# A hand-laid order of some 300 steps laid anew in a fused attention and feed-forward kernel: loads, copies and one PSUM bank with it

## The chip, the core and the metric

The kernel runs on one core of a Trainium2 chip. Its five engines run side by side, each in the order of its own instructions: TensorE (PE) multiplies matrices, VectorE (DVE) and ScalarE (ACT) work element by element, GpSimd (POOL) here issues the loads, and SyncE (SP) issues the stores and the transposes done by DMA. Semaphores order the work between them. The metric is the time of one execution on the device in microseconds; less is better.

## The reference

```
q, k, v: (4, 8, 768, 64)   n_global = 8, n_local = 96
scores = q k^T / 8 - slope[head] * dist,  kept where key < 8 or 0 <= query - key < 96
attn   = softmax(scores) v
x      = attn as (3072, 512)
h      = x @ w_in                     (512 x 2048)
out    = softplus(h) @ w_out          (2048 x 512), float32
```

Each query thus sees the eight global keys of its sequence and a band of 96 keys up to itself. `dist` is the distance, or 96 for a global key outside the band.

## The kernel before

A sequence is cut into six blocks of 128 queries; four sequences make 24 blocks. Block `n` needs the keys of its own block and of the block before. The rows of that earlier block which the band cannot reach are overwritten with the eight global keys and values (`gk`, `gv`), so that two key blocks are enough. The feed-forward part takes tiles of 256 tokens (two blocks), twelve in all, each with eight units of 256 columns of `w_in` (`f`) and eight units of the second product (`o`).

Everything is written as named steps. A step issues instructions on several engines at once, and each engine keeps the order in which the steps issue to it. The names:

- `lq`, `lk`, `lv` load a block (cast to bf16 on the way) from POOL's queue; `wi` and `wo` load weights on the same queue. `w_in` lies in five pieces (`W_IN`): units 0 and 1 alone, then 2-3, 4-5 and 6-7 together.
- `w` multiplies zeros on PE, into a bank that nobody reads. `cq`, `ck` cast the first blocks of q and k, loaded unconverted by SP's and ACT's queues.
- `t` transposes q and k of a block on PE into the bank `tr`, and DVE (or ACT, by a second number) copies them out; `tq`, `tk` do this for block 0, one tensor at a time, through the same bank. From block 8 on `d` lets the DMA transpose (SP).
- `z` writes the bias of a block (blocks 0 to 3) into the score bank by a matmul with the identity; `s` adds the scores; for later blocks `s` is followed by an addition on DVE. `e` is the exp on ACT, `p` the product with v and the division on DVE. The second number is the half of the heads.
- `x` transposes the result on PE into `XT`; `y` lets the DMA do it, on SP's queue.
- `f`: eight matmuls into one of two `hT` banks, then exp and log on ACT. `o`: four matmuls of 512 columns; every fourth is followed by DVE's copy and a store on SP.
- `g` makes POOL wait for a given unit of `f`, so that later loads are not issued too early.

The bias tables `biasA` are made by eight ACT instructions at the start (L177), ahead of every step. The first 304 steps stand in the string `ORDER`; what is left comes after it in the order of computed due times, the same in both kernels. `hT` banks come from the pool `ps2` with two buffers, which some early transposes and products share; `tr` has one.

```
nc.vector.tensor_copy(KT[n - 1][:, :, 0:NG], KT[first_of(n)][:, :, 0:NG])          # gk, L247
nc.vector.tensor_copy(v_t[n - 1][0:NG, :, 0:D], v_t[first_of(n)][0:NG, :, 0:D])    # gv, L251
```

Of the kernel before, what the change touches and what calls it, by code (L numbers as in the profile page):

```python
# [19 lines left out]
def kernel(  # L20
# [82 lines left out]
    def load_w_in(u):  # L103
        f0, f1 = u * CT, (u + W_IN[u]) * CT
        nc.gpsimd.dma_start(  # L105
            w_in_c[u][:], moe_w_in[:, f0:f1].rearrange("(m p) f -> p m f", p=P)
        )
# [64 lines left out]
    ones(2, RV)  # L172


    for half in range(2):
        for j in range(4):
            nc.scalar.mul(  # L177
                biasA[:, half, 2 * j : 2 * j + 2, :], dist_dp[:], -slopes[head_of(half, 2 * j)]
            )
# [27 lines left out]
    def tr_in(tr, j, src):
        for m in range(NPAIR):
            nc.tensor.transpose(  # L209
                tr[:, j, m, :], src[:, 2 * m : 2 * m + 2, :].rearrange("p a b -> p (a b)"), ident[:]  # L210
            )
# [8 lines left out]
    def to_KT(n, tr, copy):  # L220
        KT[n] = work4.tile(
            [P, NPAIR, P], BF16, tag="KT0" if n == first_of(n) else "KT", name="KT"
        )
        copy(KT[n][:], tr[:, 1, :, :])
# [19 lines left out]
    def gk(n):  # L244

        if n % BPB >= 2:
            nc.vector.tensor_copy(KT[n - 1][:, :, 0:NG], KT[first_of(n)][:, :, 0:NG])  # L247

    def gv(n):
        if n % BPB >= 2:  # L250
            nc.vector.tensor_copy(v_t[n - 1][0:NG, :, 0:D], v_t[first_of(n)][0:NG, :, 0:D])  # L251
# [203 lines left out]
    ORDER = """
        w16 cq0 lk1 ck0 lq1 lv0 w2 tq0 lv1 z0.1 w1 lq2 tk0 lk2 z0.0 w1 s0.0 e0.0 lk3 s0.1 t1 lv2 z1.0 lq3 p0.0
        s1.0 e0.1 lv3 z1.1 s1.1 gk2 e1.0 e1.1 t2 gk12 p0.1 p1.0 z2.0 z2.1 s2.0 p1.1 s2.1 gv2 t3 gk3 x0 wi0
        e2.0 wi1 z3.0 wi2 e2.1 x1.1 lq4 p2.0 lk4 lv4 s3.0 p2.1 z3.1 s3.1 e3.0 gv3 e3.1 wi4 x2.1 p3.0 gk4 f0
        p3.1 f1 x3 f8 f9 f2 t4 lk5 gv4 f10 s4.0 f3 lq5 f11 s4.1 wo0 f12 wi6 wo1 t5 f4 e4.0 lv5 wo2 gk5 f5
        wo3 o0 f13 o4 p4.0 e4.1 lq6 s5.0 e5.0 f6 f7 s5.1 e5.1 o1 p4.1 lk6 gv5 o5 g11 y4 g13 f14 p5.0 f15 lv6  # L460
        g7 o2 p5.1 y5 o6 o3 lk7 gk13 o7 lq7 t6 lq8 lq9 o8 lk8 s6.0 g15 e6.0 o9 o10 e6.1 lq10 t7 lv7 d8
        o11 s7.0 lk9 f16 o12 e7.0 lk10 p6.0 e7.1 d9 o13 o14 p6.1 f17 f18 y6 p7.0 o15 f19 gk8 p7.1 f20 s8.0
        lv8 f21 y7 e8.0 gk9 d10 o16 e8.1 o17 gv8 f22 p8.0 g17 s9.0 f23 o18 p8.1 gv9 gk10 e9.0 g19 lv9 f24
        f25 lq11 o19 g21 lv10 e9.1 lk11 d11 g25 f26 lv11 p9.0 s10.0 f27 p9.1 y8 g27 gk11 e10.0 e10.1 g23 o20
        o21 f28 y9 lq12 o22 gv10 f29 lq13 o23 p10.0 f30 lk12 f31 lk13 p10.1 y10 g31 s11.0 g29 gv11 e11.0 d12
        lv12 lk14 o24 e11.1 d13 o25 lq14 f32 o26 p11.0 o27 f33 p11.1 f34 o28 f35 g35 o29 y11 f36 o30 f37
        gv13 s12.0 d14 g33 o31 e12.0 e12.1 f38 p12.0 f39 lv13 s13.0 p12.1 e13.0 o32 lq15 f40 o33 e13.1 f41
        g37 gk14 y12 p13.0 lk15 g39 lk16 f42 d15 lv14 s14.0 e14.0 p13.1 gv12 f43 o34 gv14 f44 y13 lq16 e14.1
        o35 g41 g43 f45 lv15 lk17
    """  # L470
# [98 lines left out]
```

## Time and profile before

| | |
|---|---|
| median of three runs | 215.35 us (214.91 to 216.95) |
| the profiled execution | 215.15 us, of which the profile's span is 213.4 |
| PE busy | 205.5 us (96%) |
| ACT busy | 161.0 us (75%) |
| DVE busy | 109.0 us (51%) |
| POOL busy | 74.2 us (35%) |

The span runs from the first to the last instruction of the program. Of every row of a timeline the first number is the start and the second the duration, both in us; in brackets stands how long the engine was idle before it and what ended the wait. A row of the chain has start and duration, too; a row of groups has the count, the busy time, the mean in ns of one and the idle time before. A row of windows has the stretch, its length, then for each engine (PE, weight loads, DVE, ACT, POOL) its busy time and its instructions, the granted clock, the share of the DMA engines and their GB/s. L12 is line 12 of the kernel. Matmuls are pipelined, so PE starts one before the last one's duration is over.

### The profile page before, as it was taken

The numbers are of one execution on the slowest core, as the hardware profiler recorded it, in microseconds if no ns is written. First come the engines' busy times: TensorE is split into PE (matmuls) and PEld (weight loads), VectorE is DVE, ScalarE is ACT, GpSimd is POOL, SyncE is SP. The second block draws the span as 40 slices with busy tenths as digits, with TensorE's granted clock in tenths as the row PEclk, the third lists the DMA queues.
The fourth block names the chain that finished last, engine by engine and source line by source line (L and its number), as shares of the span: only waits on it lengthen the run. The fifth ranks groups of instructions, "written<-read, shape, count | busy, mean of one in ns | idle before, by whom it ended". The sixth has DMA issues, their size and how long they took to land.

```text
span 213.4 us, 4944 instructions
## 1 busy us (share of the span) xinstructions
PE 205.5 (96%) x1948; PEld 141.3 (66%) x1979; DVE 109.0 (51%) x258; ACT 161.0 (75%) x251; POOL 74.2 (35%) x116
## 2 busy tenths in 40 slices
PE   7999999999998999999999999999999999999994
PEld 2677876646766677677767766666767767666653
DVE  7595436367575656077575663465674663110121
ACT  3778999625898977799978878778878978777700
POOL 8996521880160535325552342352311000000000
PEclk9999999999999999999999999999999999999999
DMA  9999999999999999999999999999992612101112
GB/s 131 153 160 176 189 207 199 173 173 191 181 112 112 126 187 121 162 166 68 136 150 127 187 162 128 140 134 126 136 155 62 93 25 66 60 3 49 49 49 98
DMA packets 111543, 27.33 MB, mean 128 GB/s; under 512 B 103712, under 2 KB 108576, under 8 KB 111520
## 3 DMA queue, kind: packets, MB, share of 16 engines
q0 software_dynamic: 77552, 13.37, 88.2%
q1 hardware_dynamic: 32928, 13.38, 35.9%
q10 hardware_dynamic: 1040, 0.26, 0.5%
q8 instruction: 15, 0.25, 0.5%
q14 instruction: 8, 0.07, 0.1%
HBM read 27.26 MB, written 6.29 MB: 157 GB/s over the span
## 4 chain that ended last, share of the span: by engine, by line
PE 74%; DMA 15%; POOL 7%; issue 2%; DVE 0%; POOLq 0%; DVEq 0%
PE o L414 32%; PE hT L394 32%; DMA k_t<-in_k_dram 8%; DMA w_in<-in_moe_w_in_dram 5%; PE x_ps L343 4%; DMA XT<-xsf 3%; PE s_ps L260 3%; POOL q_t L99 2%; POOL k_t L99 2%; POOL v_t L99 2%; PE o L436 2%; PE s_lo L260 1%; POOL w_in L105 1%; PE tr L209 0%; POOL w_out L110 0%
## 5 line engine op out<-in xcount | busy, mean ns | idle before, releaser
L394 PE MATMUL hT<-XT,w_in 128*128 128x256 bf16 x768 | 98.3, 273 | 1.3 <-DMA XT<-xsf 0.6
L394 PEld LDWEIGHTS <-w_in 128*128 128x128 bf16 x768 | 73.6, 98 | 24.6 <-DVE XT L378 0.7
L414 PE MATMUL o<-w_out,G 128*128 128x512 bf16 x339 | 88.4, 379 | 1.5 <-issue 0.3
L399 ACT ACTIVATE e_sb<-hT 128x512 f32<-128x512 f32 x96 | 56.4, 587 | 23.2 <-PE hT L394 22.5
L400 ACT ACTIVATE G<-e_sb 128x512 bf16<-128x512 f32 x96 | 60.5, 630 | 3.6
L414 PEld LDWEIGHTS <-G 128*128 128x128 bf16 x368 | 33.0, 98 | 26.8
L327 ACT ACTIVATE Pb<-Z 128x1024 bf16<-128x1024 f32 (+1 forms) x40 | 38.9, 983 | 8.9 <-DVE Z L295 4.8
L420 DVE COPY osb<-o 128x512 f32<-128x512 f32 x23 | 15.9, 691 | 37.8 <-PE o L414 37.1
L451 POOL COPY gate_t<-G 1x1 bf16<-1x1 bf16 x32 | 5.7, 178 | 76.1 <-ACT G L400 75.7
L297 DVE TENSOR_TENSOR Z<-s_ps,biasA 128x1024 f32<-128x1024 f32 x19 | 23.2, 1221 | 11.8 <-PE s_ps L260 11.8
L354 DVE RECIPROCAL rcp<-x_ps 128x4 f32<-128x4 f32 x44 | 7.9, 180 | 30.6 <-PE x_ps L343 30.5
L99 POOL DMA_DIRECT2D v_t<-in_v_dram x24 | 21.3, 890 | 5.2 <-PE x_ps L343 2.3
L99 POOL DMA_DIRECT2D q_t<-in_q_dram x23 | 20.6, 898 | 3.5 <-issue 2.4
L99 POOL DMA_DIRECT2D k_t<-in_k_dram x23 | 20.8, 908 | 1.3 <-issue 0.9
L357 DVE TENSOR_TENSOR xsf<-x_ps,rcp 128x256 bf16<-128x256 f32 x44 | 18.7, 424 | 2.4 <-DMA XT<-xsf 0.6
L343 PEld LDWEIGHTS <-Pb 128*128 128x128 bf16 x352 | 16.7, 97 | 3.4 <-issue 0.2
L343 PE MATMUL x_ps<-v_t,Pb 128*128 128x65 bf16 x324 | 17.1, 193 | 0.0
L260 PEld LDWEIGHTS <-KT 64*128 64x128 bf16 x352 | 9.9, 94 | 6.5 <-issue 4.0
L318 DVE TENSOR_TENSOR Z<-s_lo,biasA 128x512 f32<-128x512 f32 x15 | 10.2, 679 | 0.0
L318 DVE TENSOR_TENSOR Z<-o,biasA 128x512 f32<-128x512 f32 x15 | 10.2, 679 | 0.0
L260 PE MATMUL s_ps<-QT,KT 64*128 64x128 bf16 x192 | 9.9, 219 | 0.2
L251 DVE COPY v_t<-v_t 8x512 bf16<-8x512 bf16 x16 | 7.0, 435 | 0.0
(63 smaller groups left out, 93.1 us busy)
## 6 DMA issues: line engine op xcount, KB each, us to landing
out_dram<-osb SPq DMA_DIRECT2D x23, 256.0 KB, 3.7
v_t<-in_v_dram POOLq DMA_DIRECT2D x24, 128.0 KB, 5.2
k_t<-in_k_dram POOLq DMA_DIRECT2D x23, 128.0 KB, 6.1
q_t<-in_q_dram POOLq DMA_DIRECT2D x23, 128.0 KB, 6.1
w_out<-in_moe_w_out_dram POOLq DMA_DIRECT2D x4, 512.0 KB, 14.5
w_in<-in_moe_w_in_dram POOLq DMA_DIRECT2D x3, 512.0 KB, 9.9
w_in<-in_moe_w_in_dram POOLq DMA_DIRECT2D x2, 256.0 KB, 6.0
XT<-xsf SPq DMA_TRANSPOSE x20, 4.7
```

Of the source, the lines that this page charges most:

```text
L99: nc.gpsimd.dma_start(dst[n][:, :, 0:D], src[b, :, i * P : (i + 1) * P, :].rearrange("h s d -> s h d"))
L260: nc.tensor.matmul(dst(4 * sub + 2 * mm + t), KT[n - t][rows, m, :], QT[n][rows, m, :], start=not pre, stop=not pre or (mm == 1 and (t == ...
L297: nc.vector.tensor_tensor(Z[:], s_ps[:], biasA[:, half, :, :], ALU.add)
L318: nc.vector.tensor_tensor(Z[:, regs, :], s_i[:, 0:4:step, :], bias[:, 1, regs, :], ALU.add)
L327: nc.scalar.activation(Pb[:, 0:nreg, :], src, AF.Exp, scale=inv_sqrt)
L343: nc.tensor.matmul(x_b[:, lh, :], Pb[:, r, :], v_t[n - t][:, h, :], start=(t == 0), stop=(t == 1 or first),)
L357: nc.vector.tensor_tensor(xsf[:, h0 : h0 + 4, :], x_b[:, :, 0:D], rcp[:, h0 : h0 + 4][:, :, None].to_broadcast([P, 4, D]), ALU.mult,)
L394: nc.tensor.matmul(hT[:, j, :], w[:, m, fo : fo + P], XT[c][:, m, :], start=(m == 0), stop=(m == KM - 1),)
L399: nc.scalar.activation(e_sb[:], hT[:], AF.Exp)
L400: nc.scalar.activation(G[c][:, 2 * u : 2 * u + 2, :], e_sb[:], AF.Ln, bias=1.0)
L414: nc.tensor.matmul(o[:], G[c][:, 4 * kq + a, ns * P : ns * P + P], w_out_c[kq][:, a, :], start=(kq == 0 and a == 0), stop=(kq == NWC - 1 a ...
L420: nc.vector.tensor_copy(osb[:], O.pop((c, ns))[:])
```

## The change

The steps of `ORDER` are laid anew. With that:

- units 2 and 3 of `w_in` are two pieces of 256 KB (`wi2`, `wi3`) instead of one of 512 KB;
- the ACT products for `biasA` become steps (`bb`), two at a time, put among the first steps;
- `gk` of blocks 2 and 3 is a copy on ACT, `gv` of blocks 2 and 3 a copy on POOL; `gv` copies all 65 columns of a head, the column of ones with it;
- the first K^T goes through an `hT` bank instead of `tr`;
- the steps `w2`, `w1`, `w1` are gone; `y4`, `y5` become `x4`, `x5`; the copy of `x0` goes to ACT and those of `x1` and `x2` to DVE; `t6` copies Q^T by ACT.

```diff
-    W_IN = {0: 1, 1: 1, 2: 2, 4: 2, 6: 2}
+    W_IN = {0: 1, 1: 1, 2: 1, 3: 1, 4: 2, 6: 2}
...
-    for half in range(2):
-        for j in range(4):
+    def bias_part(half, part):
+        for j in range(2 * part, 2 * part + 2):
...
-            nc.vector.tensor_copy(KT[n - 1][:, :, 0:NG], KT[first_of(n)][:, :, 0:NG])
+            copy_by(n < NPB)(KT[n - 1][:, :, 0:NG], KT[first_of(n)][:, :, 0:NG])
...
-            nc.vector.tensor_copy(v_t[n - 1][0:NG, :, 0:D], v_t[first_of(n)][0:NG, :, 0:D])
+            copy = (nc.gpsimd if n < NPB else nc.vector).tensor_copy
+            copy(v_t[n - 1][0:NG], v_t[first_of(n)][0:NG])
...
-        w16 cq0 lk1 ck0 lq1 lv0 w2 tq0 lv1 z0.1 w1 lq2 tk0 lk2 z0.0 w1 s0.0 e0.0 lk3 s0.1 t1 lv2 z1.0 lq3 p0.0
-        s1.0 e0.1 lv3 z1.1 s1.1 gk2 e1.0 e1.1 t2 gk12 p0.1 p1.0 z2.0 z2.1 s2.0 p1.1 s2.1 gv2 t3 gk3 x0 wi0
-        e2.0 wi1 z3.0 wi2 e2.1 x1.1 lq4 p2.0 lk4 lv4 s3.0 p2.1 z3.1 s3.1 e3.0 gv3 e3.1 wi4 x2.1 p3.0 gk4 f0
-        p3.1 f1 x3 f8 f9 f2 t4 lk5 gv4 f10 s4.0 f3 lq5 f11 s4.1 wo0 f12 wi6 wo1 t5 f4 e4.0 lv5 wo2 gk5 f5
-        wo3 o0 f13 o4 p4.0 e4.1 lq6 s5.0 e5.0 f6 f7 s5.1 e5.1 o1 p4.1 lk6 gv5 o5 g11 y4 g13 f14 p5.0 f15 lv6
-        g7 o2 p5.1 y5 o6 o3 lk7 gk13 o7 lq7 t6 lq8 lq9 o8 lk8 s6.0 g15 e6.0 o9 o10 e6.1 lq10 t7 lv7 d8
+        w16 bb1.0 cq0 ck0 bb0.0 lq1 tq0 lk1 tk0 lv0 z0.0 lk2 z0.1 s0.0 bb0.1 e0.0 lq2 bb1.1 t1 lv1 s0.1 e0.1
+        lk3 lq3 z1.0 s1.0 e1.0 p0.0 z1.1 s1.1 t2 lv2 lv3 z2.0 wi0 e1.1 wi1 p0.1 gk2 p1.0 p1.1 gv2 s2.0 z2.1
+        wi2 lq4 e2.0 s2.1 e2.1 t3 gk3 x0.1 z3.0 p2.0 p2.1 s3.0 x1 e3.0 z3.1 lk4 gv3 s3.1 x2 e3.1 p3.0 f0 lq5
+        p3.1 f1 wi3 x3 wi4 lk5 f2 wo0 lv4 wi6 gk13 f8 wo1 t4 gk4 gv4 f9 lv5 f10 wo2 s4.0 f11 f3 s4.1 wo3 f4
+        lq6 gk5 t5 e4.0 e4.1 f12 s5.0 f5 o0 o4 p4.0 s5.1 f13 p4.1 gv5 lk6 f6 lv6 e5.0 lq7 f7 x4 g7 e5.1 f14
+        o5 lq8 lk7 p5.0 o1 f15 p5.1 g13 o6 x5 lk8 o2 g15 f16 g11 o3 o7 t6.2 f17 f18 lk9 s6.0 lv7 e6.0 f19 o8
...
-        o11 s7.0 lk9 f16 o12 e7.0 lk10 p6.0 e7.1 d9 o13 o14 p6.1 f17 f18 y6 p7.0 o15 f19 gk8 p7.1 f20 s8.0
-        lv8 f21 y7 e8.0 gk9 d10 o16 e8.1 o17 gv8 f22 p8.0 g17 s9.0 f23 o18 p8.1 gv9 gk10 e9.0 g19 lv9 f24
+        t7 p6.0 lq9 lq10 e6.1 d8 g19 f20 s7.0 o9 p6.1 e7.0 lq11 o10 lk10 d9 e7.1 gk8 o11 lv8 f21 p7.0 f22 y6
+        o12 p7.1 gv8 s8.0 gk9 g21 y7 e8.0 d10 o13 o14 e8.1 g17 o15 f23 lv9 g23 p8.0 s9.0 lv10 lk11 o16 e9.0
+        p8.1 gv9 o17 gk10 y8 lk12 o18 o19 e9.1 f24 f25 s10.0 e10.0 o20 gk12 o21 p9.0 f26 f27 p9.1 gk11 o22
+        f28 gv10 f29 lq12 d11 y9 o23 e10.1 f30 p10.0 o24 g27 lq13 g25 lk13 f31 s11.0 p10.1 e11.0 o25 d12 f32
...
     def tr_first_k(n):
-        tr = qk_bank()
+        tr = ps2.tile([P, 2, NPAIR, P], BF16, tag="hT", name="tr_k")
```

More of the change, by code (lines that the diff above doesn't have):

```diff
@@ L461 @@
-        g7 o2 p5.1 y5 o6 o3 lk7 gk13 o7 lq7 t6 lq8 lq9 o8 lk8 s6.0 g15 e6.0 o9 o10 e6.1 lq10 t7 lv7 d8
-        o11 s7.0 lk9 f16 o12 e7.0 lk10 p6.0 e7.1 d9 o13 o14 p6.1 f17 f18 y6 p7.0 o15 f19 gk8 p7.1 f20 s8.0
-        lv8 f21 y7 e8.0 gk9 d10 o16 e8.1 o17 gv8 f22 p8.0 g17 s9.0 f23 o18 p8.1 gv9 gk10 e9.0 g19 lv9 f24
-        f25 lq11 o19 g21 lv10 e9.1 lk11 d11 g25 f26 lv11 p9.0 s10.0 f27 p9.1 y8 g27 gk11 e10.0 e10.1 g23 o20
-        o21 f28 y9 lq12 o22 gv10 f29 lq13 o23 p10.0 f30 lk12 f31 lk13 p10.1 y10 g31 s11.0 g29 gv11 e11.0 d12
@@ L466 @@
[L466 to L469, printed above, removed]
+        w16 bb1.0 cq0 ck0 bb0.0 lq1 tq0 lk1 tk0 lv0 z0.0 lk2 z0.1 s0.0 bb0.1 e0.0 lq2 bb1.1 t1 lv1 s0.1 e0.1
+        lk3 lq3 z1.0 s1.0 e1.0 p0.0 z1.1 s1.1 t2 lv2 lv3 z2.0 wi0 e1.1 wi1 p0.1 gk2 p1.0 p1.1 gv2 s2.0 z2.1
@@ new lines @@
+        o12 p7.1 gv8 s8.0 gk9 g21 y7 e8.0 d10 o13 o14 e8.1 g17 o15 f23 lv9 g23 p8.0 s9.0 lv10 lk11 o16 e9.0
+        p8.1 gv9 o17 gk10 y8 lk12 o18 o19 e9.1 f24 f25 s10.0 e10.0 o20 gk12 o21 p9.0 f26 f27 p9.1 gk11 o22
+        f28 gv10 f29 lq12 d11 y9 o23 e10.1 f30 p10.0 o24 g27 lq13 g25 lk13 f31 s11.0 p10.1 e11.0 o25 d12 f32
+        d13 f33 o26 gv11 lv11 g29 f34 e11.1 lv12 g31 o27 p11.0 lq14 f35 s12.0 o28 e12.0 lk14 y10 gv12 p11.1
+        f36 y11 e12.1 f37 s13.0 g33 e13.0 e13.1 gk14 o29 o30 p12.0 g35 lq15 f38 d14 lv13 o31 p12.1 f39 lk15
@@ L470 @@
+        o32 f40 g37 f41 o33 f42 p13.0 s14.0 f43 e14.0 f44 p13.1 d15 y12 o34 g39 lv14 gv13 y13 lk16 e14.1
+        lq16 g41 gv14 o35 g43 f45 lv15 lk17
     """
@@ L506 @@
         "wi": load_w_in, "wo": load_w_out, "g": gate, "w": warm, "cq": cast_q, "ck": cast_k, "tq": tr_first_q, "tk": tr_first_k,
-        "z": z,
+        "z": z, "bb": bias_part,
     }
```

## The prediction

> **What bounds the kernel now.** I read the busy shares first, then what TensorE (PE) waits for, then the chain that ended last, then the timeline of the first 21 us.
>
> ```profile
> span 213.4 us, 4944 instructions
> PE 205.5 (96%) x1948; PEld 141.3 (66%) x1979; DVE 109.0 (51%) x258; ACT 161.0 (75%) x251; POOL 74.2 (35%) x116
> ...
> PE hT L394 <- DMA XT<-xsf: 0.6, 1, 0.6
> PE hT L394 <- DVE XT L378: 0.5, 1, 0.5
> PE tr L209 <- DMA k_t<-in_k_dram: 0.3, 1, 0.3
> ...
> 20.00:43.50 23.50, 23.02 (x225) 16.88 (x228) 10.31 (x21) 20.18 (x33) 11.54 (x18) 1.00 1.65 189
> 65.20:210.40 145.20, 143.78 (x1310) 99.52 (x1332) 68.58 (x144) 112.35 (x174) 36.79 (x62) 1.00 1.06 110
> ```
>
> From 20 us on PE is the bound: three waits for data only (0.5, 0.3, 0.6 us), and in the last 145 us busy for 143.78. No order of steps shortens that part. What can be won is the time before the feed-forward matmuls (`f`, L394) flow, plus those waits. The first 21 us, steps in brackets:
>
> ```profile
> 1.20 4.02 PE L485 MATMUL x_ps<-warm_in 128*128 128x512 bf16 x9 [1.20 <-DVE v_t L91]
> 4.83 2.56 ACT L177 ACTIVATE biasA<-dist_dp 128x256 bf16<-128x256 bf16 x8 [2.30 <-DVE v_t L91]
> 5.33 0.61 PE L209 MATMUL tr<-ident,q_t 128*128 128x128 bf16 x4
> 5.30 0.81 DVE L491 CAST k_t<-k_f 128x512 bf16<-128x512 f32 x1
> 6.03 0.41 DVE L218 COPY QT<-tr 128x512 bf16<-128x512 bf16 x1
> 6.49 0.58 PE L209 MATMUL tr<-ident,k_t 128*128 128x128 bf16 x4
> 7.11 0.42 DVE L224 COPY KT<-tr 128x512 bf16<-128x512 bf16 x1 [0.67 <-PE tr L209]
> 7.92 0.60 ACT L327 ACTIVATE Pb<-s_ps 128x512 bf16<-128x512 f32 x1 [0.53 <-PE s_ps L260]
> 9.83 1.02 ACT L327 ACTIVATE Pb<-s_ps 128x1024 bf16<-128x1024 f32 x1 [0.83 <-PE s_ps L260]
> 10.75 1.02 ACT L327 ACTIVATE Pb<-oo 128x1024 bf16<-128x1024 f32 x1
> 12.88 1.02 ACT L327 ACTIVATE Pb<-s_ps 128x1024 bf16<-128x1024 f32 x1 [1.11 <-PE s_ps L260]
> 15.56 1.02 ACT L327 ACTIVATE Pb<-s_ps 128x1024 bf16<-128x1024 f32 x1
> 16.72 1.02 ACT L327 ACTIVATE Pb<-oo 128x1024 bf16<-128x1024 f32 x1
> 17.11 1.03 PE L394 MATMUL hT<-XT,w_in 128*128 128x256 bf16 x8
> 20.01 2.79 PE L394 MATMUL hT<-XT,w_in 128*128 128x256 bf16 x24 [0.52 <-DVE XT L378]
> ```
>
> Here PE is not the bound: an alternation sets the pace, scores on PE, exp on ScalarE (ACT), next scores. The exps of blocks 1 to 3 run from 9.83 to 17.74, and ACT waits 0.83 and 1.11 us in them. `f0` starts at 17.11, `f8` at 20.01. Under all this lies the load queue:
>
> ```profile
> 10.15 2.31 POOL L105 DMA_DIRECT2D w_in<-in_moe_w_in_dram  x3
> ...
> w_in<-in_moe_w_in_dram POOLq DMA_DIRECT2D x2, 256.0 KB, 6.0
> ...
> w_in<-in_moe_w_in_dram POOLq DMA_DIRECT2D x1, 512.0 KB, 8.1
> ...
> 14.96 9.87 DMA w_in<-in_moe_w_in_dram
> 27.13 16.33 DMA k_t<-in_k_dram
> ```
>
> The two small pieces, issued at 10.15 and 10.89, land near 16.0 and 17.2; the big third, issued at 11.6, lands 8.1 later, at 19.7; the fourth at 14.96 + 9.87 = 24.8; k of block 6 at 27.13 + 16.33 = 43.46. Between the third and the fourth piece (5.1 us) lie q4, k4 and v4; less the 2.5 of a big piece that is 0.87 a block.
>
> **The change, part by part.**
>
> *First K^T through another bank.* Before, K's transposes (6.49) wait for the copy of Q^T (6.03 to 6.44), which holds the one bank `tr`. Afterwards they start when k is cast (5.30 + 0.81 = 6.11), about 6.2, and the copy at 7.11 starts at about 6.87. First scores and the exp at 7.92 come 0.24 us earlier: 7.68.
>
> *Biases.* The same eight ACT products of 0.32 (2.56/8), now in pairs. Six are over by 4.83 + 1.92 = 6.75, ahead of the first exp; the last pair (0.64) now stands between the exps of block 0 and puts the second at 8.8 instead of 8.41, which delays nothing: it ends at 9.4, just as block 1's scores are ready.
>
> *The chain of exps.* Transposes of block 1 follow the earlier first scores, so its exp starts at 9.38 instead of 9.83 (ACT free, scores there). Block 1's second follows at the pitch of the rows (10.75 - 9.83 = 0.92): 10.30. Before, block 2's scores stood behind four bias matmuls and two copies; now two of those matmuls come later, and with gk2 (below) its exp starts at 12.07 instead of 12.88. Block 3's start at 14.75 and 15.67 instead of 15.56 and 16.72, the last 1.05 earlier. `p3.0` and `f0` follow the exp that ends at 15.77: `f0` at 16.1, just after its weights (16.0).
>
> *Global copies.* gk2 and gk3 go to ACT, gv2 and gv3 to POOL. No row shows either form.
>
> ```profile
> 28.82 0.16 DVE L247 COPY KT<-KT 128x32 bf16<-128x32 bf16 x1
> 13.72 0.62 DVE L251 COPY v_t<-v_t 8x512 bf16<-8x512 bf16 x1
> 28.14 0.18 POOL L451 COPY gate_t<-G 1x1 bf16<-1x1 bf16 x1
> 15.70 1.03 POOL L99 DMA_DIRECT2D k_t<-in_k_dram  x1
> ```
>
> On ACT: between 0.16 (the same copy on DVE) and 0.32 (an ACT product eight times as wide, above); 0.25, and it is in the chain above. At 0.32 the exps of block 3 slip by 0.14, at 0.16 they come 0.18 earlier. On POOL: between 0.18 (one element) and 1.03 (its longest instruction); I take 0.6, DVE's own worst. gv2 waits for `p1.1` (11.7) and is over by 12.5; `p2.0` needs it at 13.9: hidden by 1.4 us. Behind it queue `wi2`, `lq4`, `lk4`, each 5 us or more ahead of its landing, so no transfer notices. gv3 follows `lk4` at 15.0 and ends at 15.6, 0.2 before `p3.0`; at 1.03 it costs 0.2 us, at 0.18 nothing is gained. On the copy of 128x32 this case shows 0.39 on DVE at 10.59 while POOL issues loads, against 0.16 alone:
>
> ```profile
> 10.59 0.39 DVE L247 COPY KT<-KT 128x32 bf16<-128x32 bf16 x1 [0.62 <-PE oo L260]
> ```
>
> The Trainium skill (SBUF — State Buffer, "SBUF: two separate sides") says VectorE and GpSimd share one port pair as an exclusive lock, so that whichever comes second is held up whole, while ScalarE has ports of its own. The 0.39 against 0.16 agrees. By that rule gk on ACT is the safe half, and gv on POOL would wait for a DVE copy of 0.42 at times: 1.0 instead of 0.6, which is the upper bound already taken.
>
> *Second quarter of w_in in two pieces.* Half of the 512 KB lands halfway between 17.2 and 19.7: 18.5. So `f2` can fill the time in which PE waited for the copy of `x3`: `f0` 16.1, `p3.1`, `f1` 17.2 (weights 17.2), `x3` 18.15, `f2` 18.55, `f8` 19.45 to 20.3. Before, `f8` ended at 20.88 without `f2`, a unit of 0.87. Lead: 0.56 + 0.87 = **1.43 us**. The other half (`wi3`) goes behind q4, k4 and q5, lands near 22.4 (18.5 + 3 x 0.87 + 1.25), and `f11`, its first user, comes at 22.8.
>
> *Up to the transposes of block 6.* The order follows the landings closely (unit by unit at 0.87, an `o` 0.86): t4 20.3 against k4 at 18.5 + 2 x 0.87 = 20.3, f4 24.9 against the fourth piece at 24.8. ACT, busy 20.18 of the 23.5 us from 20 on (window row above), has the same units and exps there and starts them about a us sooner; two units must wait 0.1 to 0.2 for one of the two hT banks, against the 0.16 that PE lost in that stretch before beside the wait for k (23.50 - 23.02 - 0.32). XT of blocks 4 and 5 now comes from PE, each four transposes of 128 columns, 0.22 by the L414 rate below (512 columns in 0.215): **-0.45 us**. And `f16`, which stood after t7, now comes before t6, which PE reaches near 42.8; k of block 6 needs the same bytes before it, but no longer the two DMA transposes of those blocks. So the wait ahead of 43.51 (from 42.80 + 0.22 = 43.0 on) goes: **+0.4 us**.
>
> ```profile
> 42.80 0.39 PE L209 MATMUL tr<-ident,q_t 128*128 128x128 bf16 x4
> 43.51 0.40 PE L209 MATMUL tr<-ident,k_t 128*128 128x128 bf16 x4 [0.32 <-DMA k_t<-in_k_dram]
> 56.38 0.41 PE L343 MATMUL x_ps<-v_t,Pb 128*128 128x65 bf16 x8
> 58.64 6.44 DMA XT<-xsf
> 67.13 0.86 PE o L414 x4
> ```
>
> *f24.* It waits for y7, landed at 58.64 + 6.44 = 65.08, 8.7 us after `p7.1` (56.38). Between the two stood four `f`, three `o`, two blocks' scores and `p8` (1.8): 7.9 us of PE work; the new order has one `f` and seven `o` there: 0.87 + 7 x 0.86 + 1.8 = 8.7. So that wait goes: **+0.6 us**.
>
> *The warm matmuls* after w16 go (`w2`, `w1`, `w1`); they lie in gaps of PE, so 0 if the clock stays as it is. The rest of the order only exchanges units from 65 us on; `t6.2` moves one copy from DVE (51% busy) to ACT; gv on DVE now also copies the ones column, DVE work under PE's. 0.
>
> Sum: 1.43 - 0.45 + 0.4 + 0.6 = 2.0 us. The profiled execution took 215.15 (span 213.4 and 1.75 around it), 0.2 below the median of the three runs shown (215.35): 215.15 - 2.0 = **213.1 us**.
>
> **Rivals.**
>
> *1. The clock opens later: 213.8.*
>
> ```profile
> 6.16 0.42 PE L485 MATMUL x_ps<-warm_in 128*128 128x256 bf16 x1
> 7.24 0.27 PE L485 MATMUL x_ps<-warm_in 128*128 128x256 bf16 x1
> ```
>
> The same matmul takes 0.42 at 6.16 and 0.27 at 7.24; the nine at the start take about 0.43 each for 512 columns, the later ones of L414 0.215. So PE starts at half rate and goes to full near 7.2. Without w2 and w1 it idles 0.7 us ahead of 5.33 and 0.4 after it. If it goes to full only when block 1 is through (10.4), that block's transposes, biases and scores take twice as long, and its exps come 0.5 and 0.8 later: 0.7 lost. The Trainium skill (TensorE: Matmul & The Clock Gate, Part 1) has it that the clock opens after a busy window of some 3.4 us, free-running. By that rule the 1.1 us of idle time may or may not spoil the window, and no run here shows which.
>
> *2. The wait at f24 moves to f32 and f40: 214.2.*
>
> ```profile
> XT<-xsf SPq DMA_TRANSPOSE x20, 4.7
> ```
>
> From `p9.1` to `f32` and from `p11.1` to `f40` the new order has four `f`, four `o`, one block's scores and one `p` (8.1 us of PE work), where before 9.9 and 11.4 stood. With the 8.7 us that y7 took from `p7.1` on, 0.6 is lost at each, 1.1 in all: 213.1 + 1.1 = 214.2. For it: the 6.44 us. Against it: the median landing is 4.7 us.
>
> *3. Better: 212.3.* Copies at their low bounds and no hT wait give 0.8 more.
>
> *4. Slower: PE stays at half rate until the `f` steps.* Between 7.4 and 15.9 the new order has about 7.8 us of PE work at full rate. At half rate a stretch of L us loses L/2 less the 0.6 of slack; past L = 5.2, with the clock closed beyond 12.4, more than the 2.0 is lost. Closed until 17.4, when `f0` is through: 10.2/2 - 0.6 = 4.5 lost, 215.15 - 2.0 + 4.5 = 217.7. For it: sparser PE work than before; against it: at half rate PE would be busy nearly all the time.
>
> **How the numbers follow.** Forecast 0.50 (its own range 212.4 to 213.8), better 0.14, rival 1 0.09, rival 2 0.10, slower 0.17. A measurement of this kernel can tell about 1% from no change, 213.2 on the median: over half of the forecast (0.32) and all of the better case lie below, faster 0.46; the rest and rivals 1 and 2 make 0.37; slower 0.17. Range 212.0 to 217.5: it holds the low bounds and all but the worst of the slow case.
>
> **What would show it.** Right: K's transposes near 6.2, the last exp of block 3 near 15.7, `f0` near 16.1, L394 without a break to 20.3, no PE wait on k_t or XT. Wrong: 512-column matmuls at 0.43 after 7.2; POOL copies over 1 us with `p3.0` behind them; PE waiting for w_in near 18.5 or 22.5; new waits of L394 on XT between 65 and 100 us.

## The result, and the profile after

The changed kernel takes 213.71 us (median of 11 runs, 213.02 to 216.08) against 215.35 (11 runs, 214.02 to 216.95): the ratio is 0.9942, with the interval 0.9913 to 0.9970. A second measurement of the same kernel in another set of runs gave 0.9938 (0.9903 to 0.9973). The gain is some 0.6%, shown, and a little over half of the bound of 1% that the prediction set for "faster". The profiled execution took 213.65, with a span of 211.9; before it was 215.15 and 213.4. All ratios leave out one slow run, 240.11 us with the global values copied by DVE, at a granted clock of 0.85.

The head of the page of the changed kernel, and what PE waits for in it (line numbers beyond L248 are one higher than before):

```profile
span 211.9 us, 4946 instructions
PE 204.1 (96%) x1952; PEld 140.6 (66%) x1984; DVE 108.2 (51%) x256; ACT 162.0 (76%) x253; POOL 75.9 (36%) x119
```
```profile
PE x_ps L486 <- DVE v_t L91: 1.2, 1, 1.2
PE tr L209 <- DVE q_t L489: 0.5, 1, 0.5
PE o L415 <- issue: 0.5, 3, 0.2
PE tr_k L209 <- DVE k_t L492: 0.4, 1, 0.4
```

The three waits for data that stood in the middle of the kernel before (XT by DMA, XT by DVE, k_t) are gone; what is left lies in the first 6.2 us, or is one of three pauses of at most 0.2 us ahead of an `o`. The first 20 us as a timeline:

```profile
5.31 0.80 DVE L492 CAST k_t<-k_f 128x512 bf16<-128x512 f32 x1
5.33 0.40 PE L209 MATMUL tr<-ident,q_t 128*128 128x128 bf16 x4 [0.54 <-DVE q_t L489]
...
6.16 0.40 PE L209 MATMUL tr_k<-ident,k_t 128*128 128x128 bf16 x4 [0.44 <-DVE k_t L492]
...
7.40 0.60 ACT L328 ACTIVATE Pb<-s_ps 128x512 bf16<-128x512 f32 x1 [0.62 <-PE s_ps L261]
...
9.20 1.02 ACT L328 ACTIVATE Pb<-s_ps 128x1024 bf16<-128x1024 f32 x1
...
11.12 0.21 ACT L247 COPY KT<-KT 128x32 bf16<-128x32 bf16 x1
11.79 0.61 POOL L252 COPY v_t<-v_t 8x520 bf16<-8x520 bf16 x1
12.19 1.02 ACT L328 ACTIVATE Pb<-s_ps 128x1024 bf16<-128x1024 f32 x1 [0.86 <-PE s_ps L261]
...
16.16 1.02 ACT L328 ACTIVATE Pb<-oo 128x1024 bf16<-128x1024 f32 x1
16.73 1.05 PE L395 MATMUL hT<-XT,w_in 128*128 128x256 bf16 x8
18.02 1.05 PE L395 MATMUL hT<-XT,w_in 128*128 128x256 bf16 x8
```

K^T's transposes follow the cast of k, and the exps up to block 2 come within 0.3 us of where they were expected. But `f0` starts at 16.73 and `f1` at 18.02, and the chain that ended last says why the next unit is no earlier:

```profile
11.79 0.57 POOL v_t L252
12.36 6.96 DMA w_in<-in_moe_w_in_dram
19.32 0.05 issue
19.36 1.92 PE hT L395 x16
```

The third piece of `w_in` lands at 12.36 + 6.96 = 19.32, and `f2` follows at 19.36. From there on no wait of PE for data is long enough to be listed. That makes the start of the third `f` unit the candidate for what sets the end: from it to the start of `f46` (103.87) are 84.51 us here. The experiments test this.

Where the 1.6 us at `f46` came from (the spans differ by 1.5), in PE's rows. First before, then after, at the transposes of block 6, at `f24` and at `f46`:

```profile
43.51 0.40 PE L209 MATMUL tr<-ident,k_t 128*128 128x128 bf16 x4 [0.32 <-DMA k_t<-in_k_dram]
43.74 1.03 PE L414 MATMUL o<-w_out,G 128*128 128x512 bf16 x4
...
65.22 0.60 PE L394 MATMUL hT<-XT,w_in 128*128 128x256 bf16 x4 [0.55 <-DMA XT<-xsf]
...
105.47 0.71 PE L394 MATMUL hT<-XT,w_in 128*128 128x256 bf16 x5
```
```profile
43.70 0.39 PE L209 MATMUL tr<-ident,k_t 128*128 128x128 bf16 x4
43.92 1.25 PE L395 MATMUL hT<-XT,w_in 128*128 128x256 bf16 x10
...
64.48 1.25 PE L395 MATMUL hT<-XT,w_in 128*128 128x256 bf16 x10
...
103.87 1.04 PE L395 MATMUL hT<-XT,w_in 128*128 128x256 bf16 x8
```

The kernels do not stand at the same work at these points, so a unit done besides counts as its 0.87 (an `f`) or 0.86 (an `o`).

| point | before | after | done besides | lead | this stretch | predicted |
|---|---|---|---|---|---|---|
| end of `f8` | 20.88 | 21.12 | `f2` | 0.63 | +0.63 | +1.43 |
| end of block 6's transposes | 43.74 | 43.92 | `f16` | 0.69 | +0.06 | -0.05 |
| start of `f24` | 65.22 | 64.48 | `o19` | 1.60 | +0.91 | +0.60 |
| start of `f46` | 105.47 | 103.87 | none | 1.60 | 0 | 0 |

The start is worth less than predicted by 0.8, the stretch up to `f24` more by 0.3.

### The profile page after: what moved, and what is told of

Read it like the earlier page. It is cut to its first block, busy times and chain, and to the rows that moved or that the text cites. A ratio compares the mean times of both kernels' runs of the same rounds, so it can differ in the third digit from the quotient of the medians.

```text
span 211.9 us, 4946 instructions
## 1 busy us (share of the span) xinstructions
PE 204.1 (96%) x1952; PEld 140.6 (66%) x1984; DVE 108.2 (51%) x256; ACT 162.0 (76%) x253; POOL 75.9 (36%) x119
## 3 DMA queue, kind: packets, MB, share of 16 engines
HBM read 27.26 MB, written 6.29 MB: 158 GB/s over the span
## 4 chain that ended last, share of the span: by engine, by line
PE 90%; DMA 5%; issue 1%; DVE 1%; POOL 0%
PE hT L395 39%; PE o L415 37%; PE x_ps L344 5%; PE s_ps L261 4%; DMA w_in<-in_moe_w_in_dram 3%; DMA k_f<-in_k_dram 2%; PE o L437 2%; PE s_lo L261 2%; PE tr L209 1%; DVE k_t L492 0%; DVE KT L224 0%; POOL v_t L252 0%; PE tr L376 0%; PE s_ps L283 0%; DVE QT L218 0%
## 5 line engine op out<-in xcount | busy, mean ns | idle before, releaser
L358 DVE TENSOR_TENSOR xsf<-x_ps,rcp 128x256 bf16<-128x256 f32 x44 | 18.7, 424 | 1.5
L261 PE MATMUL o<-QT,KT 64*128 64x128 bf16 x66 | 6.6, 216 | 0.0
```

What stands on the lines that cost most here:

```text
L261: nc.tensor.matmul(dst(4 * sub + 2 * mm + t), KT[n - t][rows, m, :], QT[n][rows, m, :], start=not pre, stop=not pre or (mm == 1 and (t == ...
L358: nc.vector.tensor_tensor(xsf[:, h0 : h0 + 4, :], x_b[:, :, 0:D], rcp[:, h0 : h0 + 4][:, :, None].to_broadcast([P, 4, D]), ALU.mult,)
```

## The experiments

The theory to be tested: the start of the third `f` unit sets the end, and the queue of loads sets that start, not the chain of exps; the later order of steps keeps the lead. Its rivals: the copies on POOL hold up the loads queued behind them; the chain of exps or the clock is the bound; the lead comes from one part of the order alone. "Start of f2" and the landings are in the table behind the experiments.

**The kernel again, nothing changed.**

> The changed kernel once more, to see how far the landings of the load queue and the steps of the first 21 us differ between executions. Theory 1 (the queue sets f0, f1 and f2, and it is as slow as this in every execution): w_in pieces land near 16.7, 18.0 and 19.3 us again, f2 starts within 0.2 us of 19.4. Rival (the landings of the one profile were a late draw): they land near 16.0, 17.2 and 18.5 and f2 starts near 18.6. Ratio to the kernel before 0.992 to 0.997.

Measured: 214.33 us, ratio 0.9938 (0.9903 to 0.9973). In its profile the exps come 0.5 us sooner than in the first execution, because DVE's cast of k took 0.40 us and not 0.80:

```profile
5.21 0.40 DVE L492 CAST k_t<-k_f 128x512 bf16<-128x512 f32 x1
...
15.66 1.02 ACT L328 ACTIVATE Pb<-oo 128x1024 bf16<-128x1024 f32 x1
```
```profile
12.47 6.96 DMA w_in<-in_moe_w_in_dram
19.43 0.05 issue
19.48 1.92 PE hT L395 x16
```

The last exp at 15.66 rather than 16.16, and `f2` still at 19.48: half a us in the chain of exps buys nothing. That speaks for the queue, whose pieces land at 16.76, 18.10 and 19.43, as the theory had them.

**Global values of blocks 2 and 3 copied by DVE.**

```diff
-            copy = (nc.gpsimd if n < NPB else nc.vector).tensor_copy
+            copy = nc.vector.tensor_copy
```

> The changed kernel with the gv copies of blocks 2 and 3 back on VectorE. Theory 1 (the load queue is slow for its own reasons): w_in pieces land as before within 0.2 us, f2 near 19.4, time the same within 0.3 us of the changed kernel. Rival (the two copies on POOL, 0.61 us each, and the wait ahead of the first hold up the issue and so the transfers): the third piece is issued at 11.6 instead of 12.36 and the pieces land 0.6 to 0.8 us earlier, f2 near 18.6, time 0.6 to 0.8 us less.

Measured: 214.66 us, ratio 0.9956 (0.9920 to 0.9991). The chain:

```profile
11.89 8.29 DMA w_in<-in_moe_w_in_dram
20.18 0.05 issue
20.23 1.92 PE hT L395 x16
```

With POOL free of the copy the third piece is issued 0.47 sooner (11.89 against 12.36), yet lands 0.86 later. What came late was the queue itself: its first piece landed at 17.61 (16.68 in the changed kernel), and from that to the third it took 2.57 against 2.64. So the copy on POOL does not hold the loads here, and the rival's 0.6 to 0.8 us did not come.

**The second quarter in one piece, twice.**

```diff
-    W_IN = {0: 1, 1: 1, 2: 1, 3: 1, 4: 2, 6: 2}
+    W_IN = {0: 1, 1: 1, 2: 2, 4: 2, 6: 2}
```

> The changed kernel with units 2 and 3 of w_in in one piece of 512 KB again, loaded where wi2 stands. Theory 1 (f2 waits for its weights): the piece lands 1.2 us after the small one did, near 20.6; f2 starts 1.2 us later and TensorE does not get it back, so the time is 0.9 to 1.3 us more than the changed kernel's, close to the kernel before. Rival (another wait, such as the copy of x3 or a bank of hT, ends last at f2): f2 moves by less than 0.4 us and the time by less than 0.4.

Measured: 214.37 us, ratio 0.9975 (0.9942 to 1.0007), with `f2` at 19.36 in the profile, the very time of the split kernel. By that profile alone the split would be worth nothing, so the kernel was run once more:

> The changed kernel with the second w_in quarter as one load of 512 KB again, in a new execution. In the first one it landed at 19.32, as the third of the small pieces did in the changed kernel. Theory A (splitting is worth nothing, the last of the sixteen completion marks decides either way): f2 starts at 19.2 to 19.6, f46 84.5 us later, ratio to the kernel before within 0.003 of the changed kernel's 0.994. Theory B (the first execution was a lucky draw, a whole piece lands as late as in the kernel before plus the later issue, near 20.5): f2 at 20.5, f46 at 105.0, time 0.9 to 1.2 us above the changed kernel's.

Measured: 214.35 us, ratio 0.9974 (0.9952 to 0.9997). The first profile has the row of the changed kernel (12.36, 6.96), the second these:

```profile
12.45 7.86 DMA w_in<-in_moe_w_in_dram
20.31 0.05 issue
20.36 1.92 PE hT L395 x16
```

The same load lands at 19.32 and at 20.31. The difference is there before it: the first piece, issued at 10.14 and 10.41, took 5.1 us in the first run and 6.0 in the second (it landed at 15.20 and 16.43). These are the rows of the DMA issues, cut to the moment of that one issue; below them is the same row of the kernel before (issued at 10.15, landed at 15.87) and of the changed one (10.14, 16.68):

```profile
w_in<-in_moe_w_in_dram POOLq DMA_DIRECT2D x1, 256.0 KB, 5.1
```
```profile
w_in<-in_moe_w_in_dram POOLq DMA_DIRECT2D x1, 256.0 KB, 6.0
```
```profile
w_in<-in_moe_w_in_dram POOLq DMA_DIRECT2D x1, 256.0 KB, 5.7
```
```profile
w_in<-in_moe_w_in_dram POOLq DMA_DIRECT2D x1, 256.0 KB, 6.5
```

Ten loads in the same places of the queue stand before it each time. So the landing of the first piece varies by over a us from one execution to the next, and the later ones follow it. From the first to the third landing the time varies less: 2.57 to 2.69 with the split in the seven profiles that load v of block 0 by POOL's queue, and 3.84 to 4.12 with the whole quarter in four of five. The exception is the first late-only run below (4.93), whose second piece had fifteen of its sixteen completion marks (see the last section) by 16.31 and the last at 18.20. Measured from its own first landing, the split thus brings the landing that `f2` waits for some 1.2 to 1.5 us forward. In the times it shows as 0.0034 of the ratio (0.9975 and 0.9974 against 0.9942 and 0.9938), 0.7 us; the intervals overlap, so the size of that is rough.

**Without the load of v of block 3.**

```diff
-    v_t = [v_r[n % RV] for n in range(NB)]
+    v_t = [v_r[2 if n == 3 else n % RV] for n in range(NB)]
...
-        lk3 lq3 z1.0 s1.0 e1.0 p0.0 z1.1 s1.1 t2 lv2 lv3 z2.0 wi0 e1.1 wi1 p0.1 gk2 p1.0 p1.1 gv2 s2.0 z2.1
+        lk3 lq3 z1.0 s1.0 e1.0 p0.0 z1.1 s1.1 t2 lv2 z2.0 wi0 e1.1 wi1 p0.1 gk2 p1.0 p1.1 gv2 s2.0 z2.1
```

> The changed kernel without the load of v of block 3 (block 3 and its neighbour use the values of block 2 in its place), so that every later load moves up by one block. Theory 1 (the queue is what f0, f1 and f2 wait for): the w_in pieces land 0.8 to 0.9 us earlier (near 15.8, 17.1, 18.4), f0 starts near 16.3, set by the exp chain, f2 0.8 us earlier, and the time falls by 0.6 to 0.9 us. Rival (the chain of exps on ScalarE sets f0 to f2): the pieces land earlier, f0 to f2 stay within 0.2 us, the time within 0.3.

Measured: 213.31 us, ratio 0.9895 (0.9862 to 0.9929). PE's rows:

```profile
18.12 0.39 PE L376 MATMUL tr<-ident,xsf 128*128 128x128 bf16 x4
18.44 1.92 PE L395 MATMUL hT<-XT,w_in 128*128 128x256 bf16 x16
```

A load of 128 KB fewer in front of `w_in`, and `f2` starts at 18.44, `f46` at 102.95: 0.92 us sooner, all of it kept to the end (span 211.0). `f2` follows the landing (18.40) and the end follows `f2`: in this stretch the queue is the bound. That the missing load is what brought the landing forward, one profile can't show, since its first landing (15.71) lies inside the spread of those with all ten loads; the times speak for it (0.9895 against 0.9942 and 0.9938), though the intervals overlap a little.

**v of block 0 by SP's queue.** It is loaded unconverted there and cast by ACT, after the first exp.

```diff
+    v_f = const.tile([P, H, D], F32, name="v_f")
+    nc.sync.dma_start(v_f[:], v[0, :, 0:P, :].rearrange("h s d -> s h d"))
...
+    def cast_v(n):
+        nc.scalar.copy(v_t[n][:, :, 0:D], v_f[:])
```

> The changed kernel with v of block 0 loaded unconverted on SyncE's queue behind q, and cast by ScalarE after the first exp; POOL's queue has one block less ahead of the weights. Theory 1 (f0 to f2 wait for the queue, and the first 4 us of the DMA engines have room): w_in pieces land about 0.8 us earlier, f2 at 18.5 to 18.8, time 0.6 to 0.9 us below the changed kernel's, like the kernel without v of block 3. Rival (the DMA engines are the limit already while q and k of block 0 arrive): the cast q and k come later or POOL's first blocks do, and the pieces land within 0.3 us of where they did; time the same within 0.3.

Measured: 213.36 us, ratio 0.9922 (0.9898 to 0.9945). The first piece lands at 15.05, the third at 18.23, yet `f2` starts at 19.12. ACT's rows show the other bound, which is now the later one:

```profile
7.41 0.60 ACT L330 ACTIVATE Pb<-s_ps 128x512 bf16<-128x512 f32 x1 [0.63 <-PE s_ps L263]
7.90 0.61 ACT L497 CAST v_t<-v_f 128x512 bf16<-128x512 f32 x1
...
16.59 1.02 ACT L330 ACTIVATE Pb<-oo 128x1024 bf16<-128x1024 f32 x1
```

The last exp is 0.43 later than in the changed kernel, `f0` comes at 16.90, and `f1` and `f2` follow without a wait for `w_in`. Here `f2` starts 2.53 after the last exp, with `w4` and with the cast on DVE 2.52 after it. By that the last exp of the changed kernel (16.16) would let `f2` start near 18.7, an estimate: down to there the queue is the bound, below it the chain of exps. The median is the lowest of all that keep the whole computation, but the intervals overlap with the changed kernel's: that it is faster is not shown.

**The same with the cast on DVE.**

```diff
-        nc.scalar.copy(v_t[n][:, :, 0:D], v_f[:])
+        nc.vector.tensor_copy(v_t[n][:, :, 0:D], v_f[:])
```

> As the run with v of block 0 on SyncE's queue, but VectorE casts it (before p0.0) rather than ScalarE, so that the chain of exponentials is not lengthened by the cast. Theory (queue first, then the chain of exponentials): pieces land 1 us earlier than in the changed kernel (15.1, 16.4, 18.3), the exponentials are at most 0.3 later, f2 starts at 18.7 to 18.9, f46 at 103.2 to 103.4, the median 0.3 to 0.6 below the changed kernel's. Rival: the later landing of q and k of block 1 sets the exponentials, they are 0.4 later as before, f2 stays near 19.1 and the time is the changed kernel's within 0.2.

Measured: 213.83 us, ratio 0.9966 (0.9948 to 0.9984): no better than the changed kernel. Eight of its twelve runs lie within 0.03 us (213.81 to 213.84), three between 214.68 and 214.82, and one at 215.84, which is the profiled one. Its profile is therefore not the usual run. In it the clock opened only at 9.6 us (4.80 in the changed kernel), the last exp starts at 17.46, `f2` at 19.98 (its piece had landed at 18.57), and later one wait of 1.07 us is added, for a DVE division whose buffer a DMA transpose still read:

```profile
63.05 0.42 DVE L360 TENSOR_TENSOR xsf<-x_ps,rcp 128x256 bf16<-128x256 f32 x1 [1.90 <-DMA XT<-xsf]
```
```profile
63.53 0.40 PE L346 MATMUL x_ps<-v_t,Pb 128*128 128x65 bf16 x8 [1.07 <-DVE xsf L360]
```

The expected 18.7 for `f2` was missed in this profile; whether the usual run has it stays open.

**The clock: `w4` instead of `w16`.**

```diff
-        w16 bb1.0 cq0 ck0 bb0.0 lq1 tq0 lk1 tk0 lv0 z0.0 lk2 z0.1 s0.0 bb0.1 e0.0 lq2 bb1.1 t1 lv1 s0.1 e0.1
+        w4 bb1.0 cq0 ck0 bb0.0 lq1 tq0 lk1 tk0 lv0 z0.0 lk2 z0.1 s0.0 bb0.1 e0.0 lq2 bb1.1 t1 lv1 s0.1 e0.1
```

> The changed kernel with four units of warm matmuls (two instructions) in place of sixteen, so that TensorE idles from about 2 us to 5.3 us. Theory (the clock opens by activity in the time before, as the rivals of the prediction have it): it opens only after 8 us, the transposes and biases of block 1 run at half rate (106 ns for 128 columns), exps of block 1 0.4 to 0.9 us later. Whether that reaches the end: f0 to f2 wait for the load queue in any case, with 0.6 us of slack at f0, so the time rises by 0 to 0.4 us. Rival (opening does not depend on these matmuls): full rate by 7.2 us, nothing moves.

Measured: 214.34 us, ratio 0.9984 (0.9944 to 1.0023). The clock opened at 8.75 and the exps came 0.6 later:

```profile
16.75 1.02 ACT L328 ACTIVATE Pb<-oo 128x1024 bf16<-128x1024 f32 x1
```

Its third piece landed early (18.96), and `f2` started at 19.27 right behind `f1`, so this profile's end is that of the changed kernel (`f46` at 103.81). The median lies higher by 0.4%, but the interval does not tell it from the changed kernel. Inconclusive in the time; in the profile an opening at 8.75 makes the chain of exps as late as the queue was in the changed kernel (19.36), and 0.3 later than this run's own queue.

**`f8` ahead of `f2`.**

```diff
-        p3.1 f1 wi3 x3 wi4 lk5 f2 wo0 lv4 wi6 gk13 f8 wo1 t4 gk4 gv4 f9 lv5 f10 wo2 s4.0 f11 f3 s4.1 wo3 f4
+        p3.1 f1 wi3 x3 wi4 lk5 f8 wo0 lv4 wi6 gk13 f2 wo1 t4 gk4 gv4 f9 lv5 f10 wo2 s4.0 f11 f3 s4.1 wo3 f4
```

> The changed kernel with f8 ahead of f2, the order of the kernel before. f8 needs the first quarter of w_in and the copy of block 3's transposed x, which ends near 19.7 in the changed kernel. Theory (the start of the third f unit sets the end): f8 starts at 19.8, f2 at 21.0, the end 0.4 us later than the changed kernel's (span 212.3). Rival (PE loses nothing, since f8 fills the wait for the third piece): f8 starts at 19.2 or earlier and the end is the same or up to 0.2 earlier.

Measured: 214.62 us, ratio 0.9973 (0.9946 to 1.0000).

```profile
20.03 1.16 PE L395 MATMUL hT<-XT,w_in 128*128 128x256 bf16 x9 [0.52 <-DVE XT L379]
```

The third unit starts at 20.03, behind the copy of `x3` as before the change, and `f46` at 104.54, again 84.51 later. The end is 0.67 later than in the changed kernel (0.4 expected; its first landing was 0.18 later, too). So by this profile the split pays because `f2` stands in front of `f8`.

**The new order only up to the transposes of block 6**, then the old one.

```diff
-        o5 lq8 lk7 p5.0 o1 f15 p5.1 g13 o6 x5 lk8 o2 g15 f16 g11 o3 o7 t6.2 f17 f18 lk9 s6.0 lv7 e6.0 f19 o8
+        o5 lq8 lk7 p5.0 o1 f15 p5.1 g13 o6 x5 lk8 o2 g15 f16 g11 o3 o7 t6.2 gk12 lq9 o8 s6.0 e6.0 o9 o10 e6.1
...
```

> The changed kernel up to the step t6.2, and after it the steps that are left in the order of the kernel before. Theory (the gain has two parts: about 0.85 us up to t6, and about 0.75 us where f24 no longer waits for y7): TensorE is 0.85 us ahead at t6, XT of block 7 again lands after TensorE reaches f24, which waits 0.3 to 0.7 us; span 212.4 to 212.9, ratio to the kernel before 0.994 to 0.998. Rival (all of the gain is made before t6 and kept, the wait at f24 was only the draw of one profile): no wait at f24, span near 212.0.

Measured: 214.99 us, ratio 1.0008 (0.9980 to 1.0035): nothing is left of the gain. `f2` starts at 19.37 and block 6's transposes come as in the changed kernel, then:

```profile
45.23 0.28 PE L261 MATMUL s_ps<-QT,KT 64*128 64x128 bf16 x4 [0.27 <-DVE KT L224]
...
49.68 1.02 PE L415 MATMUL o<-w_out,G 128*128 128x512 bf16 x3 [0.30 <-DVE osb L421]
...
52.68 1.58 PE L395 MATMUL hT<-XT,w_in 128*128 128x256 bf16 x13
```

`f17` starts at 52.68; in the kernel before it was 52.65. The lead of 0.69 is gone in 9 us, 0.57 of it in the two waits shown. With `f16` already done nothing stands between block 6's transposes and its scores but one `o`, and between the `o` units nothing that would cover DVE's copy. The changed order puts `f17` and `f18` behind the transposes, and `f19`, `f20` and `f21` among the `o` units. The steps after 44 us keep the lead; between 44 and 65 us the prediction counts nothing of the order but the wait at `f24`. As for that wait, `f24` (64.95) waits 0.26 here, by the trace for ACT's log of an earlier unit; y7 lands only at 58.69 + 6.12 = 64.81, nearly as long after its issue as in the kernel before (6.44).

**The new order only from `p7.1` on**, in two tries.

```diff
-        p8.1 gv9 gk10 e9.0 g19 lv9 f24
+        lv8 g19 f20 lq11 f21 f22 gv8 s8.0 gk9 g21 y7 e8.0 d10 e8.1 g17 f23 ... p8.0 s9.0 ... o16 ... o18 o19 e9.1 f24
...
```

The first try had `lv8` behind `g19` and `lq11`:

> The kernel before up to the step p7.1, and after it the steps that are left in the new order, so that 8.8 us of TensorE work instead of 7.9 stand between p7.1 and f24. Theory (the wait at f24 is worth what it lasted): f24 does not wait, no new wait of TensorE on XT later, span 0.5 to 0.7 us less than the kernel before's, ratio 0.996 to 0.999. Rival (the wait moves to f32 or f40): TensorE waits there for XT and the time is that of the kernel before within 0.2 us.

Measured: 222.31 us, ratio 1.0321 (1.0269 to 1.0373).

```profile
66.00 0.60 PE L343 MATMUL x_ps<-v_t,Pb 128*128 128x65 bf16 x8 [4.69 <-DMA v_t<-in_v_dram]
```

PE waited 4.69 us for v of block 8, whose load stood behind a gate. As a test of the wait at `f24` it failed. The second try has `lv8` in front:

> The kernel before up to p7.1, with the changed kernel's order from there on (lv8 first in it): f24 has o18 and o19 and four more units between y7 and itself. Theory (the wait of 0.6 at f24 was PE time lost, and is gone with the order alone): no wait of PE ahead of f24, f46 0.5 to 0.7 earlier than before at the same start of f8, span 212.7 to 212.9 where f8 starts at 20.0. Rival: the units moved ahead of f24 wait for something else (DVE's or ScalarE's copies), f46 less the start of f8 stays at 85.4 and the time is that of the kernel before.

Measured: 216.88 us, ratio 1.0088 (1.0075 to 1.0101), slower than before.

```profile
63.41 0.41 PE L343 MATMUL x_ps<-v_t,Pb 128*128 128x65 bf16 x8 [1.34 <-DVE Z L318]
```

No wait is left at `f24`, but 1.34 us are lost at `p8.0`, which by the trace waits for DVE's sums for block 8. In the changed kernel `o13`, `o14` and `o15` stand there as cover; here they were used up before `p7.1`. From the third unit (20.50) to `f46` (107.42) it takes 86.92 us, against 85.46 before. The rival was right in kind, that the units moved ahead of `f24` bring another wait, and too mild in size: the kernel is slower than before. That the wait at `f24` alone is worth 0.6 is thus not shown; what is shown is that neither half of the order, cut at these places, gains by itself.

**All profiles side by side** (us; landings are from the trace, the last column is from the start of the third `f` unit to that of `f46`):

| kernel | first piece lands | third (or whole quarter) | from first to third | third `f` unit | `f46` | difference |
|---|---|---|---|---|---|---|
| before | 15.87 | 19.74 (whole) | 3.87 | 20.01 | 105.47 | 85.46 |
| changed | 16.68 | 19.32 | 2.64 | 19.36 | 103.87 | 84.51 |
| changed, again | 16.76 | 19.43 | 2.67 | 19.48 | 104.09 | 84.61 |
| gv on DVE | 17.61 | 20.18 | 2.57 | 20.23 | 104.74 | 84.51 |
| whole quarter | 15.20 | 19.32 (whole) | 4.12 | 19.36 | 103.88 | 84.52 |
| whole quarter, again | 16.43 | 20.31 (whole) | 3.88 | 20.36 | 104.86 | 84.50 |
| without v of block 3 | 15.71 | 18.40 | 2.69 | 18.44 | 102.95 | 84.51 |
| `w4` | 16.29 | 18.96 | 2.67 | 19.27 | 103.81 | 84.54 |
| `f8` first | 16.86 | 19.53 | 2.67 | 20.03 | 104.54 | 84.51 |
| v of block 0 by SP, ACT | 15.05 | 18.23 | 3.18 | 19.12 | 103.85 | 84.73 |
| early part only | 16.64 | 19.32 | 2.68 | 19.37 | 105.21 | 85.84 |
| v of block 0 by SP, DVE | 14.95 | 18.57 | 3.62 | 19.98 | 105.75 | 85.77 |
| late part only, first try | 15.46 | 20.39 (whole) | 4.93 | 20.04 | 112.26 | 92.22 |
| late part only, second try | 17.37 | 21.21 (whole) | 3.84 | 20.50 | 107.42 | 86.92 |

The last column shows the changed order's later part (84.50 to 84.61 in eight profiles) and what it is worth: 0.95 against the kernel before, 1.3 against the old order behind the new start. What sets the third unit shows, too. In seven profiles it starts 0.04 to 0.05 after the third landing; in three (`w4` and both with v of block 0 on SP's queue) 2.52 to 2.53 after the last exp; in those with `f8` as the third unit behind the copy of `x3`. In the row of SP and ACT fifteen of the sixteen marks of the third piece are there by 17.69 and the last comes at 18.23, hence 3.18; its later issue (12.86) does not explain it, for with `w4` the piece was issued at 12.94 and the distance is 2.67.

## Why the prediction was right, and where it was off

The total was right: 213.1 predicted, 213.71 measured, inside the range, and the sign was that of the forecast. But it was right with terms that were off in both directions: 0.8 us less at the start, 0.1 and 0.3 more later. That the later terms made up for half of the first is luck. The number alone does not tell the forecast from rival 1 (213.8), which lies nearer to it; the traces do, for the clock opened sooner here. And by the bound of 1% that the prediction set itself, 213.2, the result falls among the cases that it did not count as faster (0.37).

- *First K^T, biases, exps*: transposes at 6.16 (6.2 predicted), first exp at 7.40 (7.68), block 1 at 9.20 (9.38), block 2 at 12.19 (12.07), the last exp at 16.16 (15.67). The first step was right. The shorter alternation was not: from the first exp to the last it is 8.76 us, where the prediction has 7.99 and the kernel before took 8.80; for most of that 0.8 the prediction shows no row. The chain is early because it starts early, and part of that is luck, the clock being open at 4.80 (7.18 before). In the second execution the last exp is at 15.66, the predicted time, but by the quicker cast; its chain takes 8.75. It cost little here, as the queue was later still.
- *Global copies*: 0.21 on ACT (0.25 taken), 0.61 on POOL (0.6 taken). The loads behind them were not held up, as the run with gv on DVE shows. Right.
- *Second quarter in two pieces*: this is the term that was mis-sized, 1.43 against 0.63. The step that failed is not "lands halfway": from the first to the third landing it predicted 16.0 to 18.5, 2.5 us, and 2.57 to 2.69 came. What failed is the 16.0 itself, read off one execution ("land near 16.0 and 17.2") and carried over as if it were the order's property. It was 16.68 in the profile of the changed kernel and lies between 15.20 and 17.61 in eight executions of the new start with the same ten loads in front (the kernels changed, changed again, gv on DVE, whole quarter twice, `w4`, `f8` first, early part only), and between 15.46 and 17.37 in three of the old start. `f0` and `f1` then wait for their weights as well, and much of what the exps gained is lost. Of the 0.8 us that are missing 0.68 are this (16.68 against 16.0), and 0.14 the distance (2.64 against 2.5). One of the prediction's own signs of being wrong, PE waiting for `w_in`, did show, at 19.36.
- *Up to block 6*: -0.45 + 0.4 predicted, +0.06 measured. The wait for k is gone, the two `x` steps cost 0.23 each (start to start in PE's rows). Right to about 0.1.
- *f24*: the wait of 0.55 is gone. But the stretch gave 0.91. Counted from start to start the wait was worth 0.71: the last product of `p8.1` starts at 64.48, `f24` at 65.22, and the products before it follow each other every 0.03. The other 0.2 is not traced; the early-only run shows what kind it may be, since small waits eat the lead where `f` units no longer stand between the `o` units. That the order between block 6's transposes and `f24` is needed to keep any of the lead stands nowhere in the prediction. Its step for the rest, a mere exchange of units from 65 us on, was right: the lead is 1.60 at `f24` and at `f46`.
- *The warm matmuls* (w2, w1, w1): 0 predicted, and PE's first transposes already take 0.40 for four (0.61 before), so the clock was open sooner, not later. When it opens is a draw (see the last section), so this says nothing on what the steps that are gone are worth.
- *Rivals*: the clock a window later (rival 1) came up by chance in one execution, that of the cast on DVE, and with `w4`; in the latter it cost at most 0.3 at `f2` (19.27, the piece at 18.96). No wait turned up at `f32` or `f40` (rival 2). The better case (rival 3) did not come, as the copies took their middle values. PE at half rate until the `f` steps (rival 4) did not occur.

## What to carry to other kernels

Where the start of the dense part hangs on a queue of loads, a landing time read off one execution is a draw: take the distances between landings from the profile, but give the first one a spread, and repeat the profile before calling an experiment's result nothing. Splitting a load paid here because the order had a step ready that needs just the first half. And a lead won early has to be carried: units that only cover the small waits of others are worth as much as the wait that was taken away, and here neither half of the order could be judged alone.

## What the runs showed of the hardware

*A load lands with the slowest of sixteen marks.* In the trace each load has sixteen completion marks. For the first piece of `w_in` in the changed kernel the first comes at 14.18, the twelfth at 15.08, the last at 16.68; with gv on DVE 14.47, 15.40 and 17.61. The first marks lie within 0.45 us (14.06 to 14.50) in the eleven executions with ten loads in front, the last ones within 2.4 (15.20 to 17.61): a few of the sixteen lag, and in the changed kernel the next three pieces keep the lag (first to last mark 2.50 in the first piece, 2.31 in the fourth). In the two profiles with v of block 0 on SP's queue the spread is 0.55 and 0.8 us, and their runs agree unusually well (213.34 to 213.56 in four runs, eight of twelve within 0.03); whether the one follows from the other is not shown. What makes a mark lag is open. The Trainium skill (DMA: Bandwidth & Descriptors, "Why a DMA increments its semaphore by 16 and not by 1") says that sixteen engines finish a GpSimd load independently and that only the full sixteen mean it has landed. The trace agrees; the size of the lag is this case's.

*The same cast takes 0.40 or 0.80 us.* DVE's cast of k (128x512) starts at 5.19 to 5.21 and takes 0.40 in eight of the fourteen profiles; in the other six (before, changed, the first with the whole quarter, the first late-only one, both with v of block 0 on SP's queue) it starts at 5.26 to 5.37 and takes 0.73 to 0.85. In the eight the load that POOL issues at 4.95 takes it 1.13 or 1.14, in the six 0.89 or 0.90:

```profile
4.96 1.14 POOL L99 DMA_DIRECT2D q_t<-in_q_dram  x1
```

So in each profile one of the two loses, and never both. The Trainium skill (SBUF — State Buffer, "SBUF: two separate sides") has an exclusive lock between these two for some of VectorE's instructions, and the traces agree that one holds up the other. A cast that starts a tenth of a us later goes with a first exp that is 0.5 later (7.40 in the changed kernel, 6.91 in its second execution, the clock opening at 4.80 and 4.73).

*The clock opens at different times.* With the same sixteen warm matmuls from 1.20 us on, the granted clock in the trace is full from 3.85 to 6.29 us on in nine executions of the new start (4.80 in the changed kernel), and from 9.60 in one with few other differences. The Trainium skill (TensorE: Matmul & The Clock Gate, Part 1) has the clock open after a busy, free-running window of some 3.4 us. A phase that varies from run to run agrees with it; 3.85, only 2.65 us after the first matmul, does not. After the 4.69 us without matmuls in the first late-only run PE ran at half rate, and the row of windows for that stretch has a granted clock of 0.50:

```profile
66.00:70.70 4.70, 4.37 (x38) 2.69 (x40) 3.80 (x9) 2.05 (x2) 2.97 (x4) 0.50 1.40 89
```

In the trace the clock is at half from 64.11, 2.80 us after the last matmul's end (61.31), to 70.93. The same section of the Trainium skill says that one idle window of some 3.4 us closes the clock again; this trace agrees in kind, but the clock closed sooner.
